# DRAM copies of k and q cut into 16 outer rows and issued later, x's store moved ahead of other loads: mLSTM cell and squared-ReLU FFN

## The chip, the cores and the metric

The kernel runs on one core of a Trainium2 chip. Its time is the device time of one execution in microseconds (us); smaller is better. The engines are TensorE (PE in the profile, its weight loads PEld), VectorE (DVE), ScalarE (ACT), GpSimd (POOL) and SyncE (SP), which here does nothing but issue DMAs. All DMAs but two go through SP's queue, which issues them strictly in the order of the program.

## The reference

An mLSTM cell over 4 batches, 8 heads, 768 steps, head size 40, and then a feed-forward layer on its output, seen as 3072 tokens of 320 values (d_ff 2048):

```python
for t in range(S):
    m_new = np.maximum(f_gate[:, :, t] + m, i_gate[:, :, t])
    f_stab = np.exp(f_gate[:, :, t] + m - m_new)
    i_stab = np.exp(i_gate[:, :, t] - m_new)
    m = m_new
    C = f_stab * C + i_stab * outer(v_t, k_t)
    n = f_stab * n + i_stab * k_t
    y_t = sigmoid(o_t) * (C @ q_t) / max(|n . q_t|, 1)
x = y.transpose(0, 2, 1, 3).reshape(3072, 320)
h = np.maximum(x @ w_in, 0.0)
out = (h * h) @ w_out
```

The inputs q, k, v and the gates are float32; the two weights come as float64 and are rounded to float32 by the kernel.

## The kernel before

**Chunks.** The sequence is cut into 24 chunks of 128 steps, 6 to a batch. For a chunk `s`, `scores` multiplies k and q of all heads (PE), `weigh` makes the decay weights with an exponential (ACT), `weighted` multiplies the two into `P_sb` (DVE, line 421), `attend` multiplies `P_sb` with v (`hp`, line 446), q with the running state C (`hi`, line 432) and k with the weighted v (`dC`, line 439), and `normalise` divides and applies the output gate (`x_sb`, lines 472 to 482).

**The FFN.** Two chunks make a group of 256 tokens; there are 12 groups. `ffn1_main` and `ffn1_rest` (lines 525 and 536) multiply with `w_in`, `relu_half` (ACT, line 551) and `square_half` (DVE, line 558) make h squared into `g2`, and `ffn2` (line 565, group 0) or `ffn2_fast` (line 619, a form with fewer products) multiplies with `w_out`.

**Transposed operands.** PE wants k, q and x transposed. Up to chunk 6 (k, q) and chunk 5 (x) PE transposes them itself. From then on they are brought in as 32x32 squares by DMA and each square is turned by DVE (`turn_kq`, lines 312 and 314; `turn_squares`, line 501). For k and q this takes two steps in DRAM: `pair_up` (line 278) copies k and q of a chunk inside DRAM into `kq_rows`, ordered by the parity of the head, and `squares_in` (line 288) reads the squares from there. For x, `store_rows` writes `x_sb` to `x_rows` in DRAM (line 492), waits for it, and reads the squares back (line 494).

**Weights.** `Rounding` turns the 26 pieces of the weights into float32: `fetch` brings a raw piece (`raw`, line 179; from piece 10 on it is `w_out`), `words` reads its two halves on ACT (`mag` and `low`, lines 188 and 190), `join` works on them on DVE (lines 199 to 204) and adds on POOL (line 208), and then fetches the piece four places on into the buffer that came free.

**Order.** The program orders everything by hand. First a start, then a loop over `u` from 0 to 7 (chunks 2 to 5 beside the FFN's first layer of groups 0 and 1), then 4 parts for each chunk (`n`, with chunk `s = 6 + n // 4` and its part `at = n % 4`). A chunk's part 0 issues its scores, part 1 `attend_on`, part 2 the weights of the next chunk, and each part a quarter of one FFN layer of a group. Weight pieces are rounded in the parts 0 to 3 of chunk 6 (`n < 4`) for the last time. Each engine runs its own instructions in this order; whatever waits holds up all that stands behind it on its engine or on SP's queue.

## Time and profile before

| | |
|---|---|
| median of 3 runs | 584.97 us (584.03 to 585.05) |
| the profiled execution's own time | 583.88 us |
| its span, first to last instruction | 582.1 us |
| PE busy | 547.4 us (94%) |
| DVE busy | 329.2 us (57%) |
| ACT busy | 176.9 us (30%) |
| POOL busy | 99.6 us (17%) |
| DMA packets | 221380, 58.06 MB, under 512 B 184357 |

The span is shorter than the execution's own time by 1.8 us, which lie around the program. PE is busy nearly throughout, so what can be gained lies in the stretches where it waits, or where it works at a lower clock; the views that show these are in the prediction.

### The profile page before, as it was taken

How to read it: one execution, taken by the hardware profiler on the slowest of the kernel's cores; microseconds unless marked ns; L12 is line 12 of the kernel's file. 1: busy time of each engine (PE TensorE's matmuls, PEld its weight loads, DVE VectorE, ACT ScalarE, POOL GpSimd, SP SyncE). 2: the span in 40 equal slices, each digit the busy share in tenths (PEclk: the TensorE clock that was granted, in tenths of full speed). 3: DMA queues.
4: the chain of work that ended last, by engine and by line, in shares of the span. 5: the costliest groups of instructions: out<-in, count | busy, mean ns of one | idle time of the engine just before them, and what ended most of it. 6: DMA issues, size and time to landing. Idle time of an engine off the chain costs nothing.

```text
span 582.1 us, 9738 instructions
## 1 busy us (share of the span) xinstructions
PE 547.4 (94%) x3688; PEld 487.2 (84%) x3689; DVE 329.2 (57%) x637; ACT 176.9 (30%) x448; POOL 99.6 (17%) x117
## 2 busy tenths in 40 slices
PE   9989888894399999999999999999999999999997
PEld 5878776683368898898998998998998998988996
DVE  7679965761455735746646556645555556434441
ACT  3777645331130510432313134113224304011000
POOL 3345433311211021110121212011111110000000
PEclk9988998897579999999999999999999999999999
DMA  9996486776043626644644654554573021100000
GB/s 195 233 213 138 130 183 114 197 166 125 14 69 99 114 57 139 116 80 120 116 73 119 119 84 123 109 95 110 120 130 74 15 48 28 25 26 2 24 24 23
DMA packets 221380, 58.06 MB, mean 100 GB/s; under 512 B 184357, under 2 KB 217893, under 8 KB 221061
## 3 DMA queue, kind: packets, MB, share of 16 engines
q1 hardware_dynamic: 221236, 57.24, 47.2%
q8 instruction: 29, 0.48, 0.4%
q10 hardware_dynamic: 96, 0.20, 0.1%
q14 instruction: 19, 0.15, 0.1%
HBM read 49.84 MB, written 13.14 MB: 108 GB/s over the span
## 4 chain that ended last, share of the span: by engine, by line
PE 80%; DVE 6%; DMA 5%; ACT 4%; SPq 2%; issue 1%; POOL 1%; DVEq 0%; ACTq 0%; POOLq 0%
PE h_ps L619 29%; PE h_ps L525 23%; PE hp L446 7%; PE h_ps L536 6%; DMA raw<-in_moe_w_out_dram 4%; PE tp L409 3%; PE dC L439 3%; PE h_ps L565 3%; PE hi L432 2%; SPq L288 1%; DVE g L558 1%; DVE mag L203 1%; PE idle L688 1%; ACT W_sb L372 1%; ACT mag L188 1%
## 5 line engine op out<-in xcount | busy, mean ns | idle before, releaser
L525 PE MATMUL h_ps<-xT,w_in 128*128 128x256 f32 x768 | 179.4, 390 | 5.8 <-ACT xT L510 2.7
L525 PEld LDWEIGHTS h_ps<-xT,w_in 128*128 128x128 f32 x768 | 145.7, 194 | 30.4 <-ACT xT L510 3.1
L558 DVE TENSOR_TENSOR g<-r_sb 128x512 f32<-128x512 f32 x96 | 64.1, 727 | 72.0 <-ACT r_sb L551 72.0
L551 ACT ACTIVATE r_sb<-h_ps 128x512 f32<-128x512 f32 x96 | 49.9, 600 | 160.5 <-PE h_ps L536 157.3
L619 PE MATMUL h_ps<-w_out,g 128*128 128x160 f32 x528 | 76.9, 302 | 0.0
L619 PEld LDWEIGHTS h_ps<-w_out,g 128*128 128x128 f32 x528 | 72.5, 190 | 1.3 <-ACT r_sb L551 0.3
L372 ACT ACTIVATE W_sb<-A_bc,b_T 128x128 f32<-128x128 f32 x176 | 53.9, 395 | 5.9 <-POOL A_bc L357 5.9
L619 PE MATMUL h_ps<-T,S 128*128 128x160 f32 x352 | 51.4, 299 | 0.0
L536 PE MATMUL h_ps<-xT,w_in 64*128 64x256 f32 x384 | 49.0, 391 | 0.0
L619 PEld LDWEIGHTS h_ps<-T,S 128*128 128x128 f32 x352 | 49.0, 190 | 0.0
L446 PE MATMUL hp<-va,P_sb 128*128 128x41 f32 x368 | 47.3, 292 | 0.0
L446 PEld LDWEIGHTS hp<-va,P_sb 128*128 128x128 f32 x368 | 46.3, 204 | 0.0
L536 PEld LDWEIGHTS h_ps<-xT,w_in 64*128 64x128 f32 x384 | 34.8, 186 | 12.5 <-issue 9.2
L383 POOL TENSOR_TENSOR vw<-va,W_sb 128x328 f32<-128x328 f32 x20 | 16.3, 813 | 160.0 <-ACT W_sb L372 134.2
L439 PE MATMUL dC<-vw,kq 128*128 128x82 f32 x160 | 22.2, 284 | 19.6 <-DVE P_sb L421 19.6
L633 DVE TENSOR_TENSOR y_sb<-y_sb,h_ps 128x160 f32<-128x160 f32 x33 | 10.6, 321 | 48.9 <-PE h_ps L619 48.9
L439 PEld LDWEIGHTS dC<-vw,kq 128*128 128x128 f32 x160 | 20.6, 199 | 20.2 <-issue 19.9
L465 POOL TENSOR_TENSOR C_sb<-C_sb,Cd 128x328 f32<-128x328 f32 x16 | 14.1, 880 | 125.6 <-DVE C_sb L457 125.2
L421 DVE TENSOR_TENSOR P_sb<-tp,W_sb 128x512 f32<-128x512 f32 x46 | 29.3, 678 | 10.3 <-PE tp L409 9.8
L633 DVE TENSOR_TENSOR y_sb<-h_ps,y_sb 128x160 f32<-128x160 f32 x22 | 7.1, 325 | 45.8 <-PE h_ps L619 29.1
L409 PE MATMUL tp<-qT,kT 40*128 40x128 f32 x384 | 26.9, 279 | 1.7 <-ACT qT L400 1.7
L409 PEld LDWEIGHTS tp<-qT,kT 40*128 40x128 f32 x384 | 24.2, 187 | 5.1 <-ACT qT L400 2.4
(100 smaller groups left out, 618.1 us busy)
## 6 DMA issues: line engine op xcount, KB each, us to landing
A_bc<-a_rows SPq DMA_DIRECT2D x22, 512.0 KB
raw<-in_moe_w_out_dram SPq DMA_DIRECT2D x16, 320.0 KB
raw<-in_moe_w_in_dram SPq DMA_DIRECT2D x8, 512.0 KB
kq<-in_k_dram SPq DMA_DIRECT2D x24, 160.0 KB
va<-in_v_dram SPq DMA_DIRECT2D x24, 160.0 KB
og<-in_o_gate_dram SPq DMA_DIRECT2D x24, 160.0 KB
out_dram<-y_sb SPq DMA_DIRECT2D x24, 160.0 KB
x_rows<-x_sb SPq DMA_DIRECT2D x18, 192.0 KB
```

Source lines behind the costliest of these rows:

```text
L372: nc.scalar.activation(d["W"][:, i * n + h, :], A[i][:, h, :], AF.Exp, bias=b_T[:, b, c, i * n + h : i * n + h + 1],)
L409: nc.tensor.matmul(sc[i][:, j, :], lhsT=d["kT"][rows, j, :], rhs=d["qT"][rows, j, :], start=True, stop=True,)
L421: nc.vector.tensor_tensor(t, d["sc"][i], d["W"][:].rearrange("p (j two) t -> p j two t", two=2)[:, :, i, :], op=ALU.mult,)
L439: nc.tensor.matmul(dC[:, j].rearrange("p h d -> p (h d)"), lhsT=d["kq"][:, 0, 2 * j : 2 * j + 2, :].rearrange("p h d -> p (h d)"), rhs=d[" ...
L446: nc.tensor.matmul(hp[:, h, :], lhsT=d["P"][h % 2][:, h // 2, :], rhs=d["va"][:, h, :], start=True, stop=True,)
L525: nc.tensor.matmul(hs[i][:, n, :], lhsT=w_in[:, a, fb * P : (fb + 1) * P], rhs=xT[:, :, a, :], start=(n == 0 and a == 0), stop=False,)
L536: nc.tensor.matmul(hs[i][:, n, :], lhsT=w_in2[rows, 2 * pp + n, :], rhs=xT[rows, :, 2, :], start=False, stop=(n == 1),)
L551: nc.scalar.activation(rs[-1][:], h[:], AF.Relu)
L558: nc.vector.tensor_tensor(g4[:, :, i, :], r[:], r[:], op=ALU.mult)
L565: nc.tensor.matmul(o_ps, lhsT=st["g2", g][:, fb, j * P : (j + 1) * P], rhs=w_out[:, fb, :], start=(fb == 0), stop=(fb == NF - 1),)
L619: nc.tensor.matmul(to, lhsT=lhsT[:, p], rhs=rhs[:, p, :], start=(start and p == 0), stop=(p == NPAIR - 1), skip_group_check=True,)
L633: add = lambda to, a, b: nc.vector.tensor_tensor(to, a, b, op=ALU.add)
```

## The change

Five edits, all of them to DMAs or to the place of a transpose:

1. `pair_up` copies each of k and q of a chunk in two DMAs, one for each parity, instead of one. Each has 16 rows outermost (8 steps of 40 values from 4 heads: 16 x 4 x 320 values) where the old one had its 8 heads of 5120 values with the 2 parities outermost.
2. `pair_up(s + 3)` stands in chunk s, where it was `pair_up(s + 5)`, and behind the loads of that part; in the loop over `u`, chunks 7 and 8 are copied at `u` 5 and 7 (it was 7 and 8 at `u` 3, 9 at 5, 10 at 7).
3. The squares of q, which `load` brought with k and v four chunks ahead, come with those of k, two chunks ahead, in part 2 (`load_squares`, which replaces `load_kT`).
4. `store_rows`, `load`, `load_o` and `pair_up` stand at the end of part 1, behind its FFN work, in the order x's store, k and v, o, copies.
5. `turn_squares` of an even chunk stands in the next chunk's part 1, behind `normalise`, where it was in its own part 3.

```diff
     def pair_up(s):
         b, c = divmod(s, NB)
         for n, src in enumerate((k, q)):
-            nc.sync.dma_start(
-                kq_d[s, n].rearrange("two j t d -> two j (t d)"),
-                src[b, :, c * P : (c + 1) * P, :].rearrange("(j two) t d -> two j (t d)", two=2),
-            )
+            for i in range(2):
+                nc.sync.dma_start(
+                    kq_d[s, n, i].rearrange("j (m r) d -> m j (r d)", r=8),
+                    src[b, i::2, c * P : (c + 1) * P, :].rearrange("j (m r) d -> m j (r d)", r=8),
+                )
...
-        if s >= KQ_SQ:
-            if s < KQ_SQ + NKQ:
-                nc.gpsimd.memset(q_squares(s), 0.0)
-            squares_in(s, 1, q_squares(s))
-
-    def load_kT(s):
+
+    def load_squares(s):
+        if s < KQ_SQ + NKQ:
+            nc.gpsimd.memset(q_squares(s), 0.0)
         t = st[s]["kT"] = kT_b[s % NKT]
         squares_in(s, 0, t[:].rearrange("p j t -> p (j t)"))
+        squares_in(s, 1, q_squares(s))
...
     def attend_on(s):
         do(attend, s)
         do(normalise, s)
-        do(store_rows, s)
-        do(load_kT, s + 2)
-        do(load, s + 4)
-        do(pair_up, s + 5)
-        if 8 <= s < 20:
-            load_o(s + 4)
...
             load_A(s + 2)
-            for r in {3: (7, 8), 5: (9,), 7: (10,)}.get(u, ()):
-                pair_up(r)
...
             for r in {5: (8,), 7: (9,)}.get(u, ()):
                 load(r)
+            for r in {5: (7,), 7: (8,)}.get(u, ()):
+                pair_up(r)
...
-    load_kT(7)
+    load_squares(7)
...
         if at == 1:
             attend_on(s)
+            if s % GT == 1:
+                do(turn_squares, s - 1)
...
         if at == 2:
+            do(load_squares, s + 2)
             do(weigh_on, s + 1)
             do(turn_kq, s + 1)
-        if at == 3:
+        if at == 3 and s % GT == 1:
             do(turn_squares, s)
         if n < 4:
             while rounding.done < NEXT[8 + n]:
                 rounding.step()
+        if at == 1:
+            do(store_rows, s)
+            do(load, s + 4)
+            if 8 <= s < 20:
+                load_o(s + 4)
+            do(pair_up, s + 3)
```

SP's queue at `u` 3, where chunks 5 and 6 are loaded. In the rows `kq_rows` is the target of `pair_up`, `kq_88` and `kq_89` the tiles for k and q of chunks 5 and 6, `va` for v, `raw` a weight piece, `og` the output gate. Before:

```order
L278 DMA kq_rows<-in_k_dram 8x1x5120
L278 DMA kq_rows<-in_q_dram 8x1x5120
L278 DMA kq_rows<-in_k_dram 8x1x5120
L278 DMA kq_rows<-in_q_dram 8x1x5120
L300 DMA kq_88<-in_k_dram 128x8x40
L300 DMA kq_88<-in_q_dram 128x8x40
L300 DMA va_92<-in_v_dram 128x8x40
L300 DMA kq_89<-in_k_dram 128x8x40
L300 DMA kq_89<-in_q_dram 128x8x40
L300 DMA va_93<-in_v_dram 128x8x40
L179 DMA raw<-in_moe_w_out_dram 128x640
L322 DMA og<-in_o_gate_dram 128x8x40
```

And now:

```order
L301 DMA kq_88<-in_k_dram 128x8x40
L301 DMA kq_88<-in_q_dram 128x8x40
L301 DMA va_92<-in_v_dram 128x8x40
L301 DMA kq_89<-in_k_dram 128x8x40
L301 DMA kq_89<-in_q_dram 128x8x40
L301 DMA va_93<-in_v_dram 128x8x40
L179 DMA raw<-in_moe_w_out_dram 128x640
L322 DMA og<-in_o_gate_dram 128x8x40
```

The four copies that stood ahead of these loads are gone from here.

SP's queue in chunk 6, part 1, where the last weight piece is fetched (`x_rows` is x's store, `xT` its squares, `A_bc` the next chunk's decays). Before:

```order
L300 DMA kq_89<-in_k_dram 128x8x40
L300 DMA va_93<-in_v_dram 128x8x40
L288 DMA kq_89<-kq_rows 32x16x32
L288 DMA kq_89<-kq_rows 32x16x8
L288 DMA kq_89<-kq_rows 32x16x32
L288 DMA kq_89<-kq_rows 32x16x8
L278 DMA kq_rows<-in_k_dram 8x1x5120
L278 DMA kq_rows<-in_q_dram 8x1x5120
L179 DMA raw<-in_moe_w_out_dram 128x640
L332 DMA A_bc<-a_rows 128x8x128
```

And now:

```order
L289 DMA kq_90<-kq_rows 32x16x32
L289 DMA kq_90<-kq_rows 32x16x8
L289 DMA kq_90<-kq_rows 32x16x32
L289 DMA kq_90<-kq_rows 32x16x8
L179 DMA raw<-in_moe_w_out_dram 128x640 x3
L492 DMA x_rows<-x_sb 128x3x128
L494 DMA xT<-x_rows 32x12x32 x4
L301 DMA kq_89<-in_k_dram 128x8x40
L301 DMA va_93<-in_v_dram 128x8x40
L279 DMA kq_rows<-in_k_dram 16x4x320 x2
L279 DMA kq_rows<-in_q_dram 16x4x320 x2
```

The last raw piece stood behind x's store, k's squares, the loads and two copies, alone; now it is the third of three that go ahead of all of them.

DVE at the end of chunk 6 and the start of chunk 7 (the three `mag` rows are the last `join`, `P_sb` is chunk 7's). Before:

```order
L558 TENSOR_TENSOR g_1206<-r_sb 128x2x256 x4
L501 STREAM_TRANSPOSE xT<-xT 128x384
L199 TENSOR_SCALAR mag<-mag 128x320
L203 TENSOR_SCALAR mag<-mag 128x320
L204 SCALAR_TENSOR_TENSOR mag<-raw,mag 128x320
L421 TENSOR_TENSOR P_sb<-tp,W_sb 128x512 x2
```

And now:

```order
L558 TENSOR_TENSOR g_1196<-r_sb 128x2x256 x4
L199 TENSOR_SCALAR mag<-mag 128x320
L203 TENSOR_SCALAR mag<-mag 128x320
L204 SCALAR_TENSOR_TENSOR mag<-raw,mag 128x320
L421 TENSOR_TENSOR P_sb<-tp,W_sb 128x512 x2
```

The transpose of x (chunk 6) now stands behind `normalise` of chunk 7. The instructions of PE and ACT and their order are the same as before; on POOL only four memsets of q's squares moved.

## The prediction

> **What bounds the kernel now.** I read the page first, for where PE is not busy or not at full clock, then PE's waits, then the stretches around the longest wait, and last what SP's queue did before it. Part 2 of the page:

> ```profile
> span 582.1 us, 9738 instructions
> PE   9989888894399999999999999999999999999997
> PEclk9988998897579999999999999999999999999999
> ```

> A slice is 14.6 us. From slice 13 on PE is full and at full clock; all loss lies in the first 12, most of it in slices 10 and 11. PE's waits between 60 and 165 us (us in total, times, longest):

> ```profile
> PE dC L439 <- DVE P_sb L421: 18.6, 1, 18.6
> PE h_ps L525 <- ACT xT L510: 2.2, 1, 2.2
> PE h_ps L525 <- ACT r_sb L551: 2.1, 1, 2.1
> PE tp L509 <- DVE x_sb L481: 1.9, 1, 1.9
> PE tp L409 <- ACT qT L400: 1.7, 1, 1.7
> PE tp L396 <- DMA kq<-in_k_dram: 0.2, 1, 0.2
> ```

> One wait of 18.6 us outweighs the others. The stretches (length, then busy time of PE, PEld, DVE, ACT and POOL, the granted clock, DMA share, GB/s) show what it costs beside itself, and that nothing is lost from 177 to 513 us:

> ```profile
> 87.90:91.30 3.40, 3.40 (x10) 2.65 (x9) 3.40 (x6) 3.37 (x7) 1.91 (x2) 0.50 0.68 113
> 101.50:105.00 3.50, 3.49 (x8) 2.52 (x8) 3.33 (x9) 1.41 (x3) 1.32 (x2) 0.51 0.94 149
> 140.20:149.40 9.20, 0.00 (x0) 0.00 (x0) 0.00 (x0) 0.00 (x1) 0.00 (x0) 0.50 0.46 124
> 155.60:166.40 10.80, 10.79 (x35) 8.84 (x36) 6.60 (x13) 0.00 (x0) 2.88 (x4) 0.50 0.07 20
> 177.00:513.00 336.00, 336.00 (x2390) 309.83 (x2388) 190.06 (x382) 88.89 (x235) 43.63 (x48) 1.00 0.45 92
> ```

> From 140.2 to 149.4 no engine works at all: a DMA is waited for, and yet the DMA engines are only 46% busy. Afterwards PE works for 10.8 us at half clock. The timeline there (start, duration, instruction, idle time before it and its releaser):

> ```profile
> 139.49 0.61 SPq L278 DMA_DIRECT2D kq_rows<-in_q_dram  x1
> 140.21 0.36 SPq L179 DMA_DIRECT2D raw<-in_moe_w_out_dram  x1
> 149.40 0.48 ACT L188 ACTIVATE mag<-raw 128x320 f32<-128x320 f32 x1 [16.06 <-DMA raw<-in_moe_w_out_dram]
> 150.17 2.04 ACT L551 ACTIVATE r_sb<-h_ps 128x512 f32<-128x512 f32 x4
> 150.78 2.50 DVE L558 TENSOR_TENSOR g<-r_sb 128x512 f32<-128x512 f32 x4 [15.88 <-ACT r_sb L551]
> 154.78 1.28 DVE L421 TENSOR_TENSOR P_sb<-tp,W_sb 128x512 f32<-128x512 f32 x2
> ```

> The last weight piece is issued at 140.21; ACT has waited 16.06 us for it, with the FFN's relu queued behind; DVE's squares wait for the relu, chunk 7's P_sb stands behind the squares on DVE, and PE's dC waits for P_sb. So one late piece of weights stops everything. Why late? The chain of waits (start, us from issue to landing) has the same load three times, and SP's queue shows what the copies `kq_rows` do to whatever is issued after them:

> ```profile
> 95.81 4.21 DMA raw<-in_moe_w_out_dram
> 102.72 4.06 DMA raw<-in_moe_w_out_dram
> 140.21 9.11 DMA raw<-in_moe_w_out_dram
> ```

> ```profile
> 60.95 1.44 SPq L278 DMA_DIRECT2D kq_rows<-in_k_dram  x1
> 62.44 0.64 SPq L278 DMA_DIRECT2D kq_rows<-in_q_dram  x1
> ...
> 63.76 0.60 SPq L278 DMA_DIRECT2D kq_rows<-in_q_dram  x1
> ...
> 64.88 8.90 SPq L300 DMA_DIRECT2D kq<-in_q_dram  x1
> ...
> 79.80 0.73 SPq L179 DMA_DIRECT2D raw<-in_moe_w_out_dram  x1
> 80.57 0.43 SPq L322 DMA_DIRECT2D og<-in_o_gate_dram  x1
> ...
> 84.91 0.47 ACT L325 ACTIVATE og<-og 128x320 f32<-128x320 f32 x1 [6.87 <-DMA og<-in_o_gate_dram]
> ...
> 107.25 6.33 SPq L300 DMA_DIRECT2D va<-in_v_dram  x1
> ```

> A raw piece takes 4.1 to 4.2 us alone and 9.11 behind two copies: 4.9 us more for 320 KB, while more than half of the DMA engines' time is unused. The copies hold few engines for long, and all that follows waits behind them there. And SP itself sticks: behind the four copies of 60.9 to 64.4 us one load takes 8.90 us to issue, behind the next pair another takes 6.33. That is how the gate load of 80.57 came late for ACT (6.87 us).

> **The change part by part.** All sums are against the profiled execution: its span is 582.1 us, its own time 583.88, 1.8 us more; and that execution was 1.1 us faster than the median of the three runs, 584.97.

> *The last weight piece.* Its buffer comes free with a join; in the program's order that is the one which ends here (the row of 124.76), so the piece was issued 15 us after it could have been, with x's store, loads and two copies ahead of it. Now it stands ahead of them. What then sets PE's dC is worked out in the times of before, from these rows:

> ```profile
> 124.76 0.49 DVE L204 SCALAR_TENSOR_TENSOR mag<-raw,mag 128x320 int32<-128x320 int32 x1
> 128.80 2.00 PE L536 MATMUL h_ps<-xT,w_in 64*128 64x256 f32 x16
> 131.62 4.58 PE L565 MATMUL h_ps<-w_out,g 128*128 128x320 f32 x16
> 136.03 1.02 PE L432 MATMUL hi<-C_sb,qT 128*128 128x82 f32 x8
> 153.68 0.29 DVE L199 TENSOR_SCALAR mag<-mag 128x320 f32<-128x320 f32 x1
> 154.37 0.49 DVE L204 SCALAR_TENSOR_TENSOR mag<-raw,mag 128x320 int32<-128x320 int32 x1
> ```

> Issued at 125.3, landed 4.2 later at 129.5, through ACT's two steps (0.48 each) by 130.5; PE's FFN part ends at 130.8, so the relu no longer waits. From 130.8: first relu 0.6 (half a microsecond of 2.04 for four, and a start), squares 2.50, the last join 1.2 (153.68 to 154.86), first half of P_sb 0.64: ready at 135.7. PE meanwhile has the scores, line 565 and hi to do, until 137.05. The wait of **18.6 us** goes, with a cover of 1.3 us left. Edit 5 takes x's transpose out of this DVE chain; without that some 0.5 us of the cover would be gone.

> *The slow clock after it.* 10.8 us at a granted 0.50 do the work of 5.4: **5.4 us** more, if PE's wait is what lowered it.

> *The short waits.* 1.7 us at qT: ACT stood at the gate load of 80.57. With the copies gone from ahead of it, only seven loads stand between it and 60.95; even at 1 us each it is issued before 70. The 2.1 and the 2.2 us: PE waits for ACT's relu and xT copy, and ACT stood at raw pieces, each issued behind a stuck queue. The 0.2 is a load behind the copies. Sum **6.2 us**. The 1.9 us at x_sb is DVE's own chain and stays. The pieces of that stretch are now limited by their joins and 4.2 us of landing, four buffers deep, so ACT should find them landed.

> *Two short stretches at half clock* (87.9 and 101.5, 3.4 and 3.5 us, right behind the waits of 1.7 and 2.1 us): **3.4 us**, if they go with those waits. [...]

> *The copies themselves.* No row shows the new form. Below: nothing, or a small gain that the range holds, since ahead of the last weight piece now stand the copies of two chunks instead of five (chunks 7 to 11), and 54% of the DMA engines' time was free while the last pair ran. Above: each pair holds the queue as now. The nearest row is an ordinary 320 KB load, 4.1 us from issue to landing, queueing included; I take them as such loads, so nothing behind them sticks. Issue: four instead of two, 0.61 us each, 1.2 us of SP more a chunk. From 177 to 513 us run 16 chunks, 21 us each; SP issues 22 DMAs a chunk there, at some 0.5 to 0.6 us, 13 us, and 2.3 us for x's store to land (row with the rivals). SP has 5 us to spare; PE waits for none of it.

> *Squares and x's store.* The squares of q come two chunks ahead instead of four: some 40 us before use, so hidden; if they came a chunk late, PE would stop for some 20. Their issue waits behind a y store in odd chunks, for less than one part. x's store of chunk 7 now stands behind the first store of y, which waits for line 565's second half: at most one such part, 4.6 us late, with two such parts and a scores step as cover. I price this, and the thin cover of 1.3 us above, at **1.0 us** lost, between 0 and 3.

> Sum: 18.6 + 5.4 + 6.2 + 3.4 - 1.0 = 32.6 us. Span 582.1 - 32.6 = 549.5; its own time 551.3; as a median, 1.1 more: **552.4 us**.

> **The rivals.**

> *A piece still late.* DVE does two joins, k and q's turn, two joins, squares, a join and P_sb in a row there; it is nearly full, and the cover is 1.3 us. If the last piece again takes 9.11 instead of 4.21 us, P_sb comes 4.9 us later less the 0.3 that the landing has to spare, so PE waits 4.6 - 1.3 = 3.3 us and gets a slow stretch of 1.7: 557.4 us. For it: the copies of chunk 9 and x's store are issued right behind the piece. Against it: what is issued behind did not slow a piece in the rows above.

> [...]

> *The change doesn't do what it says.* If 16 outer rows hold the same few engines, the short waits and their slow stretches stay (9.6 us), and only the late piece is cured: 562.0 us. For it: no row shows the form. Against it: the loads of 128 rows reach 4.1 us for the same bytes.

> *Slower.* SP's queue becomes the bound of the steady stretch:

> ```profile
> SPq L494 <- DMA x_rows<-x_sb: 34.0, 15, 3.4
> ```

> (177 to 505 us: x's store is waited for 15 times, 2.3 us each.) If the new copies and moved squares made an issue cost 1.0 us, 22 of them and 2.3 are 24.3 us for a chunk of 21: 3.3 us in each of 16 chunks, 53 us more than forecast, 605 us. It decides from 0.85 us an issue on. Against it: the issues of squares and copies here take 0.61 us and less wherever SP isn't stuck.

> **How the numbers follow.** Chances: forecast 0.70, a piece still late 0.14, short slow stretches 0.08, copies unchanged 0.05, slower 0.03. The range: below, no residue and the 1.9 us gone too: 552.4 - 2.9 = 549.5, and half a microsecond for the spread of runs (584.03 to 585.05), 549. Above, to the third rival, 561. It leaves out the slower case, part of the third and some of what I have not thought of, no more than 2 in 10. Bounds of the unknown costs (0 to 3 us) lie inside. Some 0.2% is what a measurement of this kernel can tell from no change: faster 0.96, within it 0.01, slower 0.03.

> **What would show it.** Right: in the changed profile no PE wait over 2.5 us between 60 and 165 us; dC of chunk 7 starts near 128 us instead of 155.61; the granted clock stays at 1.0 from 60 us on; ACT's waits for raw fall from tens of us to a few; loads behind copies take about 4 us and no SP issue sticks for 6 or 8; PE from there to the end is as full as before, with the one wait after 177 us, 0.9 us of line 525 near 513 (its group after 166 us is below), moved to about 480.

> ```profile
> L525 PE MATMUL h_ps<-xT,w_in 128*128 128x256 f32 x576 | 131.1, 383 | 0.9 <-DVE xT L501 0.9
> ```

> Wrong: PE waits at xT or P_sb in the steady stretch; SP stuck at copies; a new wait at chunk 7; or a slow stretch of the clock with no wait ahead of it.

## The result and the profile after

The changed kernel takes 548.64 us (median of 4 runs, 548.35 to 548.97); the kernel before, beside it on the same chip, 584.5 us (583.18 to 585.05). The ratio is 0.939, with a 95% interval from 0.9372 to 0.9408. The profiled execution has an own time of 548.35 us and a span of 546.6 us. It is faster by 35.9 us; 32.6 were forecast, and the time lies 3.8 us under the forecast and 0.36 us under the low end of its range.

The page of the changed kernel, its parts 2 to 4:

```profile
span 546.6 us, 9788 instructions
PE   9989899999999999999999999999999999999997
PEclk9998999999999999999999999999999999999999
PE 93%; DVE 4%; ACT 1%; issue 1%; POOL 0%; DVEq 0%; POOLq 0%
```

A slice is 13.7 us here. The hole of slices 10 and 11 is gone (each digit there is 9), and of the lower clock only slice 4 is left. PE now makes up 93% of the chain of waits. PE's waits, first between 60 and 165 us, then from 165 us to the end (us in total, times, longest):

```profile
PE tp L509 <- DVE x_sb L481: 1.9, 1, 1.9
```

```profile
PE h_ps L525 <- DVE xT L501: 0.9, 1, 0.9
```

Of the six waits between 60 and 165 us that the prediction lists, the one at x_sb is left. The same stretch by busy time (length, then PE, PEld, DVE, ACT and POOL, the granted clock, DMA share, GB/s), of the kernel before:

```profile
60.00:165.00 105.00, 78.28 (x457) 64.28 (x457) 62.01 (x124) 37.59 (x91) 28.52 (x34) 0.84 0.58 128
```

and of the changed one, with the two stretches beside it:

```profile
39.57:46.40 6.83, 6.83 (x32) 6.72 (x32) 4.54 (x12) 4.64 (x14) 4.19 (x6) 0.50 1.08 229
60.00:165.00 105.00, 103.14 (x645) 85.55 (x646) 82.30 (x155) 50.29 (x123) 34.73 (x40) 1.00 0.76 151
46.40:540.00 493.60, 490.84 (x3388) 444.46 (x3387) 294.52 (x568) 148.27 (x379) 81.14 (x89) 1.00 0.49 97
```

In the same 105 us PE gets through 645 matrix products where it got through 457, and from 46.4 us on the granted clock is 1.00. The 6.83 us at 0.50 from 39.57 us stood in the kernel before as well, from 40.10, and are untouched. The place of the late piece, in the timeline (start, duration, instruction, idle time before it and its releaser):

```profile
114.75 0.33 SPq L179 DMA_DIRECT2D raw<-in_moe_w_out_dram  x1
...
118.00 0.50 ACT L188 ACTIVATE mag<-raw 128x320 f32<-128x320 f32 x1 [0.74 <-DMA raw<-in_moe_w_out_dram]
...
119.41 2.06 ACT L551 ACTIVATE r_sb<-h_ps 128x512 f32<-128x512 f32 x4 [0.52 <-PE h_ps L536]
...
120.96 3.16 DVE L558 TENSOR_TENSOR g<-r_sb 128x512 f32<-128x512 f32 x4
...
125.16 1.28 DVE L421 TENSOR_TENSOR P_sb<-tp,W_sb 128x512 f32<-128x512 f32 x2
...
126.33 1.06 PE L439 MATMUL dC<-vw,kq 128*128 128x82 f32 x8
```

The last piece is issued at 114.75 us instead of 140.21, ACT waits 0.74 us for it instead of 16.06, and dC starts at 126.33 us instead of 155.61, without a wait. The relu at 119.41 is released by PE, no longer held by ACT. The new copies' landing times stand among the DMA issues (KB each, median us from issue to landing):

```profile
raw<-in_moe_w_out_dram SPq DMA_DIRECT2D x16, 320.0 KB, 3.3
kq_rows<-in_k_dram SPq DMA_DIRECT2D x34, 80.0 KB, 3.0
kq_rows<-in_q_dram SPq DMA_DIRECT2D x34, 80.0 KB, 2.6
```

### The profile page after: what moved, and what is told of

Its sections match the earlier page's. It is cut to its first block, busy times and chain, and to the rows that moved or that the text cites. A ratio compares the mean times of both kernels' runs of the same rounds, so it can differ in the third digit from the quotient of the medians.

```text
span 546.6 us, 9788 instructions
## 1 busy us (share of the span) xinstructions
PE 537.6 (98%) x3688; PEld 480.9 (88%) x3689; DVE 329.9 (60%) x637; ACT 176.6 (32%) x448; POOL 100.5 (18%) x117
## 4 chain that ended last, share of the span: by engine, by line
PE 93%; DVE 4%; ACT 1%; issue 1%; POOL 0%; DVEq 0%; POOLq 0%
PE h_ps L619 31%; PE h_ps L525 29%; PE h_ps L536 8%; PE hp L446 8%; PE tp L409 4%; PE dC L439 3%; PE h_ps L565 3%; PE hi L432 3%; PE idle L682 1%; PE A_ps L348 1%; ACT W_sb L372 1%; DVE mag L203 1%; PE A_ps L344 1%; PE tp L396 1%; DVE g L558 1%
## 5 line engine op out<-in xcount | busy, mean ns | idle before, releaser
L525 PE MATMUL h_ps<-xT,w_in 128*128 128x256 f32 x768 | 175.5, 384 | 1.5 <-DVE xT L501 0.9
L525 PEld LDWEIGHTS h_ps<-xT,w_in 128*128 128x128 f32 x768 | 143.4, 190 | 24.7 <-issue 3.0
L551 ACT ACTIVATE r_sb<-h_ps 128x512 f32<-128x512 f32 x96 | 49.9, 601 | 196.7 <-PE h_ps L536 193.6
L558 DVE TENSOR_TENSOR g<-r_sb 128x512 f32<-128x512 f32 x96 | 62.4, 708 | 56.5 <-ACT r_sb L551 56.5
L536 PE MATMUL h_ps<-xT,w_in 64*128 64x256 f32 x384 | 49.0, 391 | 0.0
L446 PE MATMUL hp<-va,P_sb 128*128 128x41 f32 x368 | 45.7, 286 | 0.0
L536 PEld LDWEIGHTS h_ps<-xT,w_in 64*128 64x128 f32 x384 | 34.8, 186 | 12.3 <-issue 9.0
L446 PEld LDWEIGHTS hp<-va,P_sb 128*128 128x128 f32 x368 | 44.6, 198 | 0.0
L421 DVE TENSOR_TENSOR P_sb<-tp,W_sb 128x512 f32<-128x512 f32 x46 | 29.5, 682 | 7.3 <-PE tp L409 6.8
L409 PEld LDWEIGHTS tp<-qT,kT 40*128 40x128 f32 x384 | 24.2, 187 | 3.3 <-issue 2.3
L409 PE MATMUL tp<-qT,kT 40*128 40x128 f32 x384 | 26.9, 279 | 0.0
L642 ACT COPY y_sb<-h_ps 128x160 f32<-128x160 f32 x11 | 3.2, 292 | 70.6 <-PE h_ps L619 70.6
L619 PE MATMUL h_ps<-T,g 128*128 128x160 f32 x176 | 25.7, 299 | 0.0
```

The source lines that it names most:

```text
L409: nc.tensor.matmul(sc[i][:, j, :], lhsT=d["kT"][rows, j, :], rhs=d["qT"][rows, j, :], start=True, stop=True,)
L421: nc.vector.tensor_tensor(t, d["sc"][i], d["W"][:].rearrange("p (j two) t -> p j two t", two=2)[:, :, i, :], op=ALU.mult,)
L446: nc.tensor.matmul(hp[:, h, :], lhsT=d["P"][h % 2][:, h // 2, :], rhs=d["va"][:, h, :], start=True, stop=True,)
L525: nc.tensor.matmul(hs[i][:, n, :], lhsT=w_in[:, a, fb * P : (fb + 1) * P], rhs=xT[:, :, a, :], start=(n == 0 and a == 0), stop=False,)
L536: nc.tensor.matmul(hs[i][:, n, :], lhsT=w_in2[rows, 2 * pp + n, :], rhs=xT[rows, :, 2, :], start=False, stop=(n == 1),)
L551: nc.scalar.activation(rs[-1][:], h[:], AF.Relu)
```

## The experiments

The runs fall into three groups. The kernel before took 581.66 us beside the first four experiments, on one chip; on another it took 583.01 us beside the late piece, the wait at qT and the first two kernels of the last section, and 583.15 us beside the rest. So times are compared within a group, and ratios across them. In most kernels lines are shifted by one or two against the kernel they are made from.

### Edit 1 alone: the copies spread, nothing moved

In the kernel before, only `pair_up` is changed:

```diff
-            nc.sync.dma_start(
-                kq_d[s, n].rearrange("two j t d -> two j (t d)"),
-                src[b, :, c * P : (c + 1) * P, :].rearrange("(j two) t d -> two j (t d)", two=2),
-            )
+            for i in range(2):
+                nc.sync.dma_start(
+                    kq_d[s, n, i].rearrange("j (m r) d -> m j (r d)", r=8),
+                    src[b, i::2, c * P : (c + 1) * P, :].rearrange("j (m r) d -> m j (r d)", r=8),
+                )
```

> The kernel before with edit 1 alone: the copies in 16 outer rows, all else in the old order and place. Theory A (both parts are needed: the spread frees the queue, the order brings the last weight piece early): the short waits go (some 9 us with their slow clock), but the last weight piece still stands behind x's store, squares, loads and copies, 13 us of issues behind the piece before it, so it lands near 126 us instead of 118 and PE waits 5 to 8 us at dC of chunk 7 with a slow stretch after it: 556 to 560 us. Rival B (the spread alone did it, the order is worth nothing): 548 to 551 us. Rival C (the spread does nothing for the queue): 580 us or more.

Measured: 562.66 us (561.36 to 564.35), ratio 0.9667 (0.9632 to 0.9701). PE's longest wait between 60 and 165 us (of two; the other is x_sb's), the timeline and two stretches of this kernel:

```profile
PE dC L440 <- issue: 9.7, 1, 9.7
```

```profile
126.66 0.52 SPq L179 DMA_DIRECT2D raw<-in_moe_w_out_dram  x1
130.42 0.49 ACT L188 ACTIVATE mag<-raw 128x320 f32<-128x320 f32 x1 [11.62 <-DMA raw<-in_moe_w_out_dram]
```

```profile
126.93:136.58 9.65, 0.00 (x1) 0.03 (x1) 4.71 (x10) 2.81 (x6) 0.56 (x1) 0.61 0.37 102
136.60:146.10 9.50, 9.50 (x33) 7.93 (x33) 5.35 (x12) 0.00 (x0) 2.90 (x4) 0.50 0.07 21
```

Of the short waits only the one at x_sb is left, and ACT has the last piece 3.8 us after its issue, where it took 9.11 to land. But it is still issued behind the stores, loads and copies: ACT waits 11.62 us for it, PE 9.65 us at dC, and 9.5 us at half clock follow. Spreading the copies cures the queue but not the place of the piece; the time lies 2.7 us over the theory's range, and the mechanism is the one it named.

### The order alone: the old copies in the new places

The changed kernel with the two old DMAs of 8 rows in `pair_up`, the diff above turned round.

> The changed kernel with the old copies (2 rows outermost, one DMA for k and one for q), in the new order and places. Theory A: the last weight piece comes early, so the wait of 18.6 us and its 5.4 us of slow clock are gone, but the copies of chunks 7 and 8 still hold the queue for about 6 us each, so one or two short waits with slow clock come back: 552 to 560 us, and in the steady stretch the copies cost nothing. Rival B (only the spread matters): 570 us or more. Rival C (only the order matters): 548 to 550 us.

Measured: 552.14 us (549.3 to 553.95), ratio 0.9475 (0.9427 to 0.9523). In PE's waits from 60 us to the end no relu, no qT and no copy of xT by ACT is left, though SP's queue still sticks behind the old copies:

```profile
PE h_ps L524 <- DVE xT L500: 2.8, 3, 1.0
PE tp L508 <- DVE x_sb L480: 2.3, 1, 2.3
PE dC L438 <- DVE P_sb L420: 0.6, 1, 0.6
```

```profile
83.80 0.63 SPq L278 DMA_DIRECT2D kq_rows<-in_q_dram  x1
...
85.67 8.02 SPq L179 DMA_DIRECT2D raw<-in_moe_w_out_dram  x3
```

```profile
85.67:93.69 8.02, 8.02 (x62) 6.83 (x61) 6.13 (x12) 7.36 (x19) 3.97 (x5) 1.00 0.35 85
```

Three pieces take 8.02 us to issue behind one pair of old copies, 7.07 of them the first piece alone, with the DMA engines 35% busy. But PE never stops in these 8 us: four buffers lie between a piece's issue and its use, and nothing that ACT or PE needs soon stands behind the copies. So the short waits have two sufficient cures, the order or the spread. The spread is worth some 3 us on top of the order (552.14 against 548.85 us in the next but one experiment, same chip, though the fastest run here took 549.3), as two waits at xT, one at dC and the longer wait at x_sb. Behind that last one 3.41 us ran at half clock, from 69.22 us. The time lies at the low edge of theory A's range, but the waits for ACT that the copies made before did not come back. Edit 3, the squares of q, was not run by itself, so what it is worth within the order is open.

### The end of part 1 alone

The kernel before, with x's store, the squares, loads, gate and copies of a part 1 behind its rounding; the copies old, and as many chunks ahead as before:

```diff
         do(normalise, s)
-        do(store_rows, s)
-        do(load_kT, s + 2)
-        do(load, s + 4)
-        do(pair_up, s + 5)
-        if 8 <= s < 20:
-            load_o(s + 4)
...
             while rounding.done < NEXT[8 + n]:
                 rounding.step()
+        if at == 1:
+            do(store_rows, s)
+            do(load_kT, s + 2)
+            do(load, s + 4)
+            do(pair_up, s + 5)
+            if 8 <= s < 20:
+                load_o(s + 4)
```

> The kernel before with one thing moved: x's store, squares, loads, copies and gate loads of part 1 stand behind that part's FFN work and weight rounding, as in the change; old copies, old two-step loads of squares, copies five chunks ahead. Theory A (the long wait is the one late piece): the 18.6 us and the 5.4 us go, the short waits and their slow stretches (9.6 us) stay: 559 to 562 us. Rival: another late load takes its place (the squares of chunk 7 or 8, which now come later too): 565 us or more.

Measured: 566.92 us (563.07 to 568.62), ratio 0.9729 (0.9683 to 0.9775). Four of PE's six waits between 60 and 165 us (the others: 2.3 us at x_sb, 0.4 us at line 396):

```profile
PE h_ps L525 <- ACT xT L510: 3.4, 1, 3.4
PE dC L439 <- DVE P_sb L421: 3.0, 1, 3.0
PE h_ps L525 <- ACT r_sb L551: 2.5, 1, 2.5
PE tp L409 <- ACT qT L400: 1.1, 1, 1.1
```

The wait at dC falls from 18.6 to 3.0 us by this move alone: most of it was the place of the last piece. The three waits for ACT stay, two of them longer, so they come from the copies at `u` 3 to 7, which stand where they stood. And 3.0 us remain at dC, where ACT waits 5.11 us for a raw piece (until 130.72): the place does not suffice by itself. The larger of the two expected times came out, but by a late piece again and not by the squares that the rival named.

### The transpose of x not moved

The changed kernel with `turn_squares` of even chunks back in part 3:

```diff
-            if s % GT == 1:
-                do(turn_squares, s - 1)
...
-        if at == 3 and s % GT == 1:
+        if at == 3:
             do(turn_squares, s)
```

> The changed kernel without edit 5: the transpose of an even chunk's x stands in its own part 3 again, ahead of the last join and P_sb of the next chunk. Theory A (the DVE chain has a cover of more than 0.57 us): no change, 548 to 549 us. Rival (the cover was as thin as predicted or thinner): PE waits 0.5 to 2 us at dC, 549.5 to 552 us.

Measured: 548.85 us (548.0 to 549.37), ratio 0.9426 (0.9397 to 0.9455), and no wait at dC of chunk 7. In its timeline:

```profile
124.92 0.57 DVE L501 STREAM_TRANSPOSE xT<-xT 128x384 f32<-128x384 f32 x1
...
126.50 1.28 DVE L421 TENSOR_TENSOR P_sb<-tp,W_sb 128x512 f32<-128x512 f32 x2
127.29 0.98 PE L439 MATMUL dC<-vw,kq 128*128 128x82 f32 x7
```

The transpose is back in the chain, P_sb starts 0.8 us before dC instead of 1.2, and PE still comes just in time. Edit 5 brings nothing that the ratios can tell: 0.9426 without it, 0.939 and, in a later group, 0.941 with it, and the intervals overlap.

### The last piece late again

In the changed kernel the last piece is fetched at the end of part 1, behind x's store, loads and copies (the earlier ones as they are):

```diff
             self.b.append(None)
-            self.fetch()
+            if len(self.raws) < len(pieces) - 1:
+                self.fetch()
...
             do(pair_up, s + 3)
+            if n == 1:
+                rounding.fetch()
```

> The changed kernel with one DMA moved: the last weight piece is fetched at the end of chunk 6's part 1, behind x's store, the loads and the new copies, instead of at its join. Theory (that one place made the long wait): it is issued near 124.5 us instead of 114.75, lands 3.5 us later, and P_sb follows 5.4 us after its landing: PE waits 7 to 8 us at dC of chunk 7, then works some 9 us at half clock: 560 to 563 us. Rival (the wait of before came from the old copies that stood ahead of the piece, not from its place): under 553 us.

Measured: 556.55 us (553.7 to 557.24), ratio 0.9532 (0.9506 to 0.9559), in a group where the kernel before took 583.01. The timeline and two stretches:

```profile
123.89 0.49 ACT L188 ACTIVATE mag<-raw 128x320 f32<-128x320 f32 x1 [6.06 <-DMA raw<-in_moe_w_out_dram]
...
128.83 1.28 DVE L422 TENSOR_TENSOR P_sb<-tp,W_sb 128x512 f32<-128x512 f32 x2
129.62 0.70 PE L440 MATMUL dC<-vw,kq 128*128 128x82 f32 x3 [2.55 <-issue]
```

```profile
127.07:129.62 2.55, 0.01 (x1) 0.04 (x1) 2.48 (x7) 0.00 (x0) 0.56 (x1) 1.00 0.88 198
129.84:140.08 10.24, 10.24 (x35) 8.28 (x35) 6.29 (x13) 0.00 (x0) 3.15 (x5) 0.50 0.01 2
```

The piece is issued at 120.53 us, not near 124.5 as expected, and ACT gets it at 123.89 us instead of 118.00. P_sb starts 3.7 us later than in the changed kernel and dC 3.3 us later, so the cover there is 0.4 us. PE waits 2.55 us, and then works 10.24 us at half clock, 5.1 us lost: twice the wait itself. The two are 7.7 of the 8.3 us by which the span (554.9 us) is longer than the changed kernel's. The time lies between the two expectations: a late piece does bring back wait and half clock, but the wait is shorter than the theory had it.

### A wait put in at qT

The changed kernel, with 11 copies of 128x512 by ACT that nobody uses ahead of the copy of qT at `u` 5:

```diff
                     sigmoid(r)
+                spin = ps_o.tile([P, W], F32, name="tp", tag="o_ps")
+                for _ in range(11):
+                    nc.scalar.copy(spin[:], ident[:].unsqueeze(1).to_broadcast([P, 4, P]))
```

> The changed kernel with work added on ACT alone: after the gates' sigmoids of the loop's sixth round it copies a constant into a spare bank 11 times (unused, some 6.6 us), so that chunk 5's qT comes late and PE waits at its scores by about 2.3 us, as it did before the change (1.7 us). Theory (a wait that takes over half of one 3.41 us window brings a slow window): a stretch of 3.4 us at half clock follows if the wait falls in one window, and none if it is split evenly; the time is 2.3 to 4.5 us longer. [...]

Measured: 551.71 us in one execution. Two waits of PE and what follows each:

```profile
64.47:66.81 2.34, 0.00 (x1) 0.02 (x1) 2.20 (x6) 1.09 (x2) 1.05 (x2) 1.00 1.51 148
68.51:71.92 3.41, 3.41 (x9) 2.70 (x10) 3.34 (x7) 3.33 (x11) 0.00 (x0) 0.50 1.15 192
84.42:86.55 2.13, 0.00 (x1) 0.01 (x1) 0.00 (x0) 2.10 (x5) 0.00 (x0) 1.00 0.72 147
85.57:88.99 3.42, 2.44 (x22) 2.19 (x23) 2.01 (x5) 3.42 (x9) 0.72 (x1) 1.00 0.58 98
88.99:92.40 3.41, 3.41 (x20) 2.47 (x19) 3.34 (x6) 3.38 (x9) 1.19 (x2) 1.00 0.34 96
```

The wait came as planned, 2.13 us, as long as the one of 2.12 us in the kernel before, which had 3.41 us at half clock behind it; here none follows. In the kernel before, stretches of one clock follow each other so (the clock is the third figure from the end):

```profile
40.10:46.93 6.83, 6.83 (x31) 6.56 (x31) 4.88 (x11) 5.37 (x15) 4.19 (x5) 0.50 1.16 230
46.93:87.89 40.96, 37.09 (x256) 30.52 (x256) 35.14 (x61) 23.69 (x57) 17.15 (x18) 1.00 0.61 151
87.89:91.30 3.41, 3.41 (x10) 2.66 (x9) 3.41 (x6) 3.38 (x8) 1.91 (x2) 0.50 0.68 114
91.30:101.54 10.24, 8.12 (x57) 6.72 (x55) 3.89 (x10) 4.01 (x13) 2.51 (x3) 1.00 0.58 105
101.54:104.95 3.41, 3.41 (x8) 2.49 (x8) 3.24 (x9) 1.37 (x3) 1.32 (x2) 0.50 0.95 149
104.95:139.09 34.14, 29.93 (x188) 24.64 (x187) 19.14 (x41) 11.79 (x30) 8.32 (x10) 1.00 0.72 163
139.09:166.39 27.30, 10.78 (x35) 8.85 (x36) 11.35 (x22) 2.81 (x6) 3.48 (x4) 0.50 0.21 54
```

They last 1, 2, 3, 8, 10 and 12 times 3.41 us, but for the rounding; the one from 39.57 to 46.40 of the changed kernel lasts 2 times that, and the one from 196.36 to 206.60 of the next experiment 3 times. "Windows" are here the steps of 3.41 us that are counted off in a trace from such a change; they are a division of the trace, and no run shows how the chip decides. Counted from 68.51, a border at 85.57 splits this wait into 1.15 and 0.98 us; 1.72 us of the wait at 64.47 lie in one window, in which PE still works for 1.7 us, and half clock follows. Both fit the theory; its half of a window is the author's estimate.

### Fifteen waits of three lengths

To see what a wait must have to bring half clock, the changed kernel got, in part 1 of each of the chunks 8 to 22, a wait for 2, 3 or 4 copies by ACT of which nobody needs the output:

```diff
+        if at == 1 and 8 <= s < 23:
+            spin = ps_at.tile([P, W], F32, name="spin", tag="at")
+            nc.tensor.transpose(spin[:, :P], ident[:], ident[:])
+            for r in range(2 + s % 3):
+                nc.scalar.copy(spin[:], ident[:].unsqueeze(1).to_broadcast([P, 4, P]))
+            nc.tensor.transpose(spin[:, :P], ident[:], ident[:])
         if at == 1:
             attend_on(s)
```

> The changed kernel with work added that nobody uses: in each of the chunks 8 to 22 PE must wait for 2, 3 or 4 ScalarE copies of 128x512, 15 waits of some 1.3 to 2.8 us in a stretch without other waits. Theory: a wait is followed by one stretch of 3.41 us at half clock if at least about 1.75 us of it lie in one of the windows of 3.41 us that the clock's changes mark, and by none if it is shorter or split over two windows. Rival one: the length of the wait alone decides, from about 1.7 us on, wherever it lies. [...] Time: 546.6 plus some 30 us of waits plus 1.7 us for each that is followed by half clock, 580 to 600 us of span.

Measured: 625.12 us in one execution, span 623.3, longer than the 580 to 600 us that were expected. The waits came to 29.0 us; behind them 85.3 us ran at half clock, 42.7 us lost. What followed each wait:

| wait, us | starts at us | how many of the five had half clock behind them: us behind each |
|---|---|---|
| 1.30 | 173.27, 250.96, 336.52, 417.79, 495.05 | 3: none, 6.83, 6.83, 3.41, none |
| 1.92 to 1.97 | 194.20, 278.59, 360.76, 443.75, 515.98 | 3: 10.24, 10.24, 10.24, none, none |
| 2.54 to 2.59 | 146.85, 224.97, 305.09, 391.56, 465.29 | 4: none, 10.24, 10.24, 10.24, 6.83 |

Two waits of 1.30 us, each whole inside one window (counted from 196.36), and the stretch behind each:

```profile
172.47:175.88 3.41, 2.11 (x19) 1.85 (x18) 0.41 (x2) 1.18 (x2) 0.00 (x0) 1.00 0.17 52
175.88:179.29 3.41, 3.41 (x31) 3.41 (x31) 1.73 (x4) 0.00 (x0) 1.89 (x2) 1.00 0.02 7
336.31:339.72 3.41, 2.11 (x19) 1.90 (x18) 0.82 (x2) 1.18 (x2) 0.00 (x0) 1.00 0.02 5
339.72:346.55 6.83, 6.83 (x31) 6.83 (x31) 3.15 (x9) 0.00 (x0) 1.92 (x2) 0.50 0.00 0
```

PE is busy for 2.11 us in both windows, and yet only behind the second is the clock lower. So both ideas fall as they were put: the length of a wait alone does not decide (2.54 us at 146.85 brought none, 1.30 at 336.52 brought 6.83 us at half clock), and neither does the idle share of a window alone. The 1.75 us of the theory were the author's estimate, and no run shows a limit there; in the kernel before, the wait at qT was 1.75 us long (84.64 to 86.39) and had half clock behind it from 87.89. The two windows differ in what PE does in the rest: 0.69 us of the FFN's line 619 in the first, 0.10 in the second, which is filled with the narrow products of `attend` (82 and 41 columns) instead, 0.87 us of dC (line 439) against 0.28. Whether that is what parts them no run shows. Behind the second, PE is busy for all of the 6.83 us at half clock from 339.72.

### Three waits moved

In the changed kernel, chunk 2's `weighted` stands ahead of a rounding:

```diff
                 scores(s)
+                weighted(s)
                 rounding.step()
...
-            weighted(s)
+            if u > 0:
+                weighted(s)
```

> The changed kernel with one DVE step earlier: in the loop's first round, chunk 2's P_sb stands ahead of a weight piece's rounding instead of behind it. The changed kernel still waits 1.08 us at dC there (38.07 us) and then has two windows at half clock (39.57 to 46.4), which cost 3.4 us. Theory (the slow windows come from that short wait): both go, 544 to 545 us on a chip where the changed kernel takes 548.6. Rival (they come from the light work around it, half-height scores and few rows): only the 1.1 us go, 547.5 us. Second rival: the piece that is rounded 1.3 us later stops the FFN, no gain.

Measured: 549.46 us (548.74 to 550.55), ratio 0.9422 (0.9405 to 0.9439): no gain. Its waits between 30 and 165 us:

```profile
PE tp L509 <- DVE x_sb L481: 2.4, 2, 2.3
PE h_ps L525 <- ACT r_sb L551: 2.3, 1, 2.3
```

The wait of 1.1 us at dC near 38 us is gone, and one of 2.3 us at the relu, 5 us on, has come, as the second rival had it: behind the rounding that DVE now does later, POOL masks `A_bc` later, ACT waits 5.2 us for that with its decay weights, and the relu stands behind them. The 6.83 us at half clock near 40 us are gone, but 3.41 us follow the new wait (from 45.28) and 3.41 us the wait at x_sb (from 69.18). Then two moves more on top of it: chunk 3 normalised ahead of the squares, and the last chunk's x turned ahead of the last addition to y:

```diff
-            if u == 3:
-                square_half()
-            rounding.join()
+            if u != 3:
+                rounding.join()
             normalise(s)
+            if u == 3:
+                square_half()
+                rounding.join()
...
+            if at == 3 and s == NT - 1:
+                turn_squares(s)
             ffn2_fast(g, i)
...
-        if at == 3 and s % GT == 1:
+        if at == 3 and s % GT == 1 and s < NT - 1:
             do(turn_squares, s)
```

> The run before this one, and two further waits of the changed kernel: in the loop's fourth round chunk 3 is normalised ahead of the squares and a rounding (1.86 us at x_sb, 66.09 us), and the last chunk's x is turned ahead of the last addition to y (0.90 us at 478.51). Theory: 2.8 us less than that run, 541 to 542 us. Rival (the work put behind is then late itself): no better than that run.

Measured: 545.43 us (545.2 to 545.73), ratio 0.935 (0.9335 to 0.9366). To compare it with the changed kernel on one chip, three kernels ran together: the changed kernel once more, this one once more, and the changed kernel with the last two moves without the first.

> The changed kernel itself, beside the next two on one chip, since the runs before differ by up to 3 us between chips. Expected: 0.939 of the time before, 546 to 550 us; in its profile the half clock of 6.83 us near 40 us again, and none after the 1.9 us wait near 66 us unless 1.7 us or more of that wait fall into one of the windows of 3.41 us in which the clock changes.

> The kernel with three waits moved (chunk 2's P_sb ahead of a rounding, chunk 3 normalised ahead of the squares, the last chunk's x turned ahead of the last addition), again, beside the changed kernel. Theory: it gains because the half clock of 6.83 us near 40 us is gone with the wait of 1.08 us there, and because the 1.86 and 0.9 us waits go, against new waits of 2.3 and 1.7 us: 3 us under the changed kernel, ratio 0.933 to 0.936. Rival: the earlier difference was one between chips, or a lucky position of the waits in the windows of the clock: then within 1 us of the changed kernel.

> The changed kernel with two of the three moves: chunk 3 normalised ahead of the squares, and the last chunk's x turned ahead of the last addition; chunk 2's P_sb stays behind the rounding. Theory: the waits of 1.86 and 0.9 us go, 2.0 to 2.8 us, and the half clock of 6.83 us near 40 us stays: about 546 us. Rival: the order of DVE at chunk 3 gives back a wait elsewhere, as the first move alone did: no gain, 548 to 549 us.

| kernel | median, us | ratio to before | 95% interval |
|---|---|---|---|
| changed kernel | 549.11 (548.44 to 549.72) | 0.941 | 0.9393 to 0.9427 |
| three waits moved | 545.7 (545.59 to 547.75) | 0.936 | 0.9339 to 0.9381 |
| two waits moved | 545.33 (544.04 to 547.49) | 0.9336 | 0.9319 to 0.9354 |

The two moves give 3.8 us, the first adds nothing, so the rival of a mere difference between chips falls, and so does the theory's reason that half clock near 40 us has to go for the gain. The kernel with two moves beats both the kernel before and the changed one. Its two longest waits between 30 and 165 us:

```profile
PE dC L439 <- DVE P_sb L421: 1.1, 1, 1.1
PE tp L509 <- DVE x_sb L481: 0.7, 1, 0.7
```

The half clock near 40 us stays, as it was expected to; it lasts 10.24 us in this profile (from 39.86), which is of the slowest of the five runs. In the second profile of the changed kernel it lasts 3.41 us (from 41.37), not the 6.83 expected. There the wait at x_sb, without half clock behind it in the first profile (1.86 us, split by a border at 66.88, counted from 39.57), is 2.28 us long, from 64.94 us on, lies mostly in the window from 65.27, and has half clock behind it:

```profile
65.27:68.68 3.41, 1.46 (x19) 1.28 (x19) 3.17 (x6) 1.74 (x5) 1.21 (x1) 1.00 0.99 140
68.68:72.09 3.41, 3.41 (x12) 2.67 (x9) 3.14 (x7) 3.41 (x12) 0.00 (x0) 0.50 1.08 204
```

So the same wait of the same program costs 1.9 us in one execution and 2.3 + 1.7 us in another, and the stretch near 40 us 1.7 us less. Some of the spread of a kernel's runs can come from this.

## Why the prediction was right, and where it missed

The mechanism held: the waits that were to go went, and the half clock behind them. The forecast time did not: 548.64 us lies below the range of 549 to 561 us. The step that failed is the sum, by terms that are named there.

**The last weight piece, 18.6 us: right.** The profile after shows the chain as it was worked out, each step 25 us or more earlier, and with the piece made late in the changed kernel PE waits at dC again. What of it belongs to which edit: order alone cures it but for 0.6 us, spread alone leaves 9.7, the end of part 1 alone 3.0.

**The cover of 1.3 us: too large.** It is 0.4 us. Most of the difference is the squares' 2.50 us in the working, which took 3.16 here. Nothing was lost by it, since the chain still came in time, and edit 5, which was to save 0.5 us of cover, decides nothing: without it PE comes just in time, and the runs tell no difference.

**The slow clock, 5.4 us: right in size** (the products from dC on gain 5.3 us), and it does hang on the wait: in the kernel with the late piece it is back with the wait, 5.1 us.

**The short waits, 6.2 us: they went,** but for more than one reason. The prediction took the copies' form for what decided, and priced "copies unchanged", the third rival of its range, at 562.0 us, 0.961 of the kernel before. That kernel ran: 552.14 us, 0.9475. What failed there is that rival's premise, that old copies hurt wherever they stand; moved behind the loads, with four buffers of pieces between them and ACT, they hurt little. The other half of the argument, that spread copies behave like ordinary loads, held: they land in 2.6 to 3.0 us. That the old copies hold few engines for long shows in the kernel before from 145 to 147 us, behind the pair issued at 138.83 and 139.49:

```profile
DMA packets 10, 0.12 MB, mean 62 GB/s; under 512 B 3, under 2 KB 4, under 8 KB 4
q1 hardware_dynamic: 10, 0.12, 14.4%
```

14.4% of 16 engines are 2.3 of them, and of the ten packets that start there six hold nearly all of the 0.12 MB, 20 KB each: as much as a row of 5120 values of the old form.

**The short stretches at half clock, 3.4 us: they went** in the profile after (in the second profile one of 3.41 us stands behind x_sb). So 555.8 us, the time with these 3.4 us left in, to which the prediction gave a chance of 0.08, was wrong. The stretches went with the waits of 1.75 and 2.12 us that stood right ahead of them. PE need not have stood still for all of a window: in the one of 65.27 to 68.68 us above it worked for 1.46 us of 3.41, and half clock followed.

**The residue, 1.0 us: not there.** Nothing waits at chunk 7 for x, whose store did stand behind y's.

**The sum: the step that failed.** Measured 3.8 us under the forecast, by four terms.

- The waits and the half clock, 33.6 us in the sum, gave 34.55 when PE's products are lined up between the two profiles. The waits are a little longer than their rounded rows, and at the transposes of k and q (line 396) 0.75 us went where the list had 0.2.
- The residue, 1.0 us, was 0.
- The end of the kernel, put at nothing, gave 0.97: the last store's issue is followed by 2.8 us instead of 3.7 before the span ends. No run shows why. Up to here this makes a span of 546.6 us where 549.5 was forecast.
- The step from a profiled execution to a median was put at 1.1 us, since the profiled execution of before lay that much under the median of three runs; here it is 0.3.

That last distance is no property of the kernel: in the later groups the profiled execution lies between 2.2 us above its median and 0.1 below. It should have stood in the range alone. The range's low end took the residue out and even the wait at x_sb, which stayed, but it kept the 1.1 us and had nothing for the end of the kernel or for waits longer than their rows; so it missed by 0.36 us.

**The other rivals.** No piece is late, so 557.4 us was wrong as a forecast; the kernel made so took 556.55, though with a shorter wait and a longer stretch at half clock than worked out. SP's queue did not become the bound: from 177 to 505 us it waits for DVE's x_sb, the work that it is there to serve, not for its own issues:

```profile
SPq L492 <- DVE x_sb L482: 93.9, 14, 18.3
SPq L494 <- DMA x_rows<-x_sb: 29.7, 15, 3.2
```

93.9 us of idle in 14 waits for 16 chunks, nearly 6 us a chunk: it had the 5 us to spare that the prediction counted.

**What was to be seen.** No wait over 2.5 us between 60 and 165: 1.9 is the longest. dC near 128: 126.33. Clock at 1.0 from 60 us on, ACT's waits for raw pieces a few us (0.7), the wait of 0.9 us at about 480 (478.51), no issue of SP that sticks (2.11 us is the longest after 60 us), pieces behind the copies landed in about 4 us (3.85 for the one of 86.30): all so.

## What to carry to other kernels

Before a DMA is made faster, look at what stands behind it on its queue: here the order alone was worth more (29.5 us) than the copies' form alone (19.0 us), and both together, without edit 5, gave 32.8 us on the same chip, not the sum. Count a wait of the matrix engine at more than its length where half clock can follow: here 2.55 us of wait lost 5.1 us more behind it (the late piece), and 1.30 us up to 3.4 more. And keep the distance between one profiled execution and a median out of the forecast; it belongs in the range.
